# Cross attention and a feed-forward layer: the loads and conversions of the first five steps in another order, the rows of w_out written to DRAM from step 52 on, and each m made a step ahead

## The chip, the cores and the metric

The kernel runs on one core of one Trainium2 chip. The metric is the time of one execution on the device in microseconds (us), and the time of a kernel is the median of its runs. TensorE is PE in the profile, VectorE DVE, ScalarE ACT, GpSimd POOL and SyncE SP. SP computes nothing here; it issues the transfers (DMAs) one after another, so its program order is a queue.

## The reference, cut to what matters

```python
# x (8, 8, 512, 64), state (8, 8, 32, 64), w_in (512, 2048) and w_out (2048, 512)
scores = scale * np.matmul(x, state.transpose(0, 1, 3, 2))   # softmax over the 32 states
xread = np.matmul(a, state)
scores2 = scale * np.matmul(state, x.transpose(0, 1, 3, 2))  # softmax over the 512 tokens
sread = np.matmul(a2, x)
attn_out = np.concatenate([xread, sread], axis=2)            # 8 batches x 8 heads x 544 rows x 64
...
x = attn_out.transpose(0, 2, 1, 3).reshape(B * S, H * D)     # 4352 rows of 512
h = x @ w_in
g = h - np.tanh(h)
return g @ w_out
```

The weights arrive as 64-bit floats and are used as 32-bit floats.

## The kernel before, in words

**Work and chunks.** The 4352 rows are cut into nine chunks: chunks 0 to 7 are the xread rows of the eight batches, chunk 8 is all of sread. The first product is folded: instead of a·state and then w_in, the kernel makes m = state·w_in for each batch and quarter q of the 2048 hidden columns, and then h = a·m. `Chunk.hidden(f)` (L489) makes one of the 16 hidden blocks f of a chunk in a bank of `ps_h` (two banks, tiles hps), `finish` (L508) takes tanh on ACT (t) and h - tanh(h) on DVE (t or g), and `output(f)` (L526) multiplies by block f of w_out and adds up in four banks (tiles ops). Most products are made of three passes of a high and a low half (hps at L501 to L503, ops at L556 to L558); `split` (L101 to L103) makes the halves, a cast on ACT and a subtraction on DVE. Chunk 0's first blocks use plain 32-bit passes instead (hps at L499, ops at L554).

**Weights.** A block of weights is loaded raw (`Weight.load`, L111, the DMA at L121, 512 KB) and converted in four steps (`Weight.steps`, L123): a (L132, DVE), b (L133, DVE), r (L135, ACT) and p (L136, DVE, an integer addition of a and b's words and r). w00 to w03 (raw tiles w00d to w03d) are the first quarter of w_in, w10 to w33 the others, wo0 to wo15 the rows of w_out. Six raw buffers go round. `convert_win` (L617) also writes the converted quarter to the DRAM tile wf.

**m.** For batches 0 and 1 m comes from `m_first_two(q, p)` (L159): eight matmuls into a pair of banks (tiles mps, L181), then four copies on ACT (L200) into m_first (batch 0, tiles mr0) and m_second (batch 1, tiles mr1); for q of 2 and 3 batch 0's part goes to the DRAM tile md0q (L191). For batches 2 to 7 `m_units` (L208) makes it from smr and slr, two loads of state (L211, L215, split to sms and sls), with matmuls into mps (L235) and mls (L242), and writes md20 to md73 (L250, L254). `load_m` (L257) brings an m back: the DMA mr<-md (L264) into the one buffer mr, then the split to m. `Chunk.prepare(q)` calls it.

**Order.** The first part, `step(op)` (L673) over the table SEQ (L731), is laid down one engine instruction after another in the order of the table: S the scores of batch 0 (sps), c their copy, T a transpose, M a maximum, B or q the subtraction of the maximum on DVE or on POOL (L693), E exp, Z N A sum, scaling and transpose to at, a b r p the conversion steps of w00 to w03, m the products mps of a converted block, k and R the copies to mr00 and mr10 (L725, L745), h H the two halves of a hidden block of chunk 0, X its tanh and subtraction, D a matmul on a blank tile. After it comes a loop over 64 steps st (L848): chunk 0 blocks 0 to 7, chunk 1 (all 16), chunk 0 blocks 8 to 15, chunk 2, chunk 3. In each step hidden(st + 2) stands before output(st), and tables say in which step a weight is converted (CONV, WO), an m pair made (PAIRS), a row of w_out split (SPLITS) or written to the DRAM tile wod (KEEP, `keep_row`, L801, two DMAs of 256 KB a row at L805). Between the steps a scheduler orders the instructions by their dependencies, by `issue_after` (x may only stand behind y in program order) and by `high_priority`. After step 63 come two pairs of chunks (4 and 5, 6 and 7), which read w_out back from wod (L914, tiles W0m and W1m) and its mixes from wsd, and at the end chunk 8.

**Loads at the start**, in SP's order: bdr (128 KB), xT00 and xT01 (512 KB each, batch 0's x), sps (256 KB), w00d to w03d, wo0d, w10d (512 KB each).

Of the kernel before, what the change touches and what calls it, by code (L numbers as in the profile page):

```python
# [19 lines left out]
P = 128  # L20
# [17 lines left out]
def attention_ffn(ctx: ExitStack, tc: tile.TileContext, xT, xn, bd, bh, sp, sm, sl, win, wout, xout, tout, sout):  # L38
# [66 lines left out]
    class Weight:  # L105
# [33 lines left out]
        def convert(self, dst):  # L139
            for step in self.steps(dst):  # L140
                step()
# [51 lines left out]
    freed = [None]  # L193

# [61 lines left out]

    def load_m(b, q):  # L257
# [219 lines left out]
    class Chunk:  # L477
# [11 lines left out]
        def hidden(self, f):  # L489
# [7 lines left out]
            for k in range(nk):  # L497
# [133 lines left out]
    later = sorted([(s, 0, x) for s, x in zip(CONV, range(10))] + [(s, 1, x) for s, x in zip(WO, range(1, NFF))])  # L631
    loads = iter(w0[0] + wos[:1] + w0[1][:2] + [wos[x] if w else rest[x] for _, w, x in later])
# [17 lines left out]
    EARLY = int('0')  # L650
# [22 lines left out]
    def step(op):  # L673
# [18 lines left out]
        elif k in "Bq":  # L692
            o((nc.gpsimd if k == "q" else nc.vector).tensor_sub(e3(j), e3(j), ms[j].broadcast_to([P, 16, 32])))  # L693
# [7 lines left out]
        elif k in "Nw":  # L701
            o((nc.gpsimd if k == "w" else nc.vector).tensor_mul(e3(j), e3(j), zs[j].broadcast_to([P, 16, 32])))
# [3 lines left out]
        elif k in "abrp":  # L706
            if j not in csteps:
                if j % 2 == 0:
                    wb[j // 2] = pool.tile([P, 2, 512], F32, tag="wf", name=f"w00{j}", bufs=WB)
                csteps[j] = w0[0][j].steps(wb[j // 2][:, j % 2])  # L710
            x = csteps[j]["abrp".index(k)]()
            if x is not None:
                o(x)
            if k == "p":
                load(1)
                w = wb[j // 2][:, j % 2].rearrange("p (r f) -> p r f", r=4)
# [14 lines left out]
        elif k == "X":  # L731
            t = hts[j] = pool.tile([P, 512], F32, tag="t", name=f"t0_{j}", bufs=TB)
            a = nc.scalar.activation(t, hps[j], AF.Tanh)
            g = chunks[0].g[j] = pool.tile([P, 512], F32, tag="g", name=f"g0_{j}", bufs=GB)
            d = nc.vector.tensor_sub(g, hps[j], t)
            o(a)
            o(d)
            tanhs.append((a.ins, d.ins))
        elif k == "R":

            if j == 0:
                m_second[0] = second(0)
            with tc.issue_after(tanhs[RE[j]][0]):
                for c in range(2):
                    nc.scalar.copy(m_second[0][64 * c : 64 * c + 64, :, j * P : j * P + P], mps[j][64:128, c::2])  # L745

    MP = [{"a": ps_a, "o": ps_o}[x] for x in 'oaoa']
    RE = json.loads('[1, 0, 0, 1]')
    SEQ = 'S0 c0 T0 S1 D D M0 c1 q0 a0 r1 T1 D D r0 a1 E0 M1 b0 q1 E1 p0 D Z0 b1 D N0 Z1 p1 A0 N1 m0 k0 D m1 a2 k1 A1 r2 a3 h0 H0 h1 H1 b3 b2 p2 X0 X1 m2 r3 D p3 m3 k2 D k3'
# [3 lines left out]
    for j in range(4):  # L753
        step(f"R{j}")
    FILL = json.loads('[1, 0, 1, 2]')
    afters = [firstDVE[0], tanhs[0][1], tanhs[1][1]]
# [29 lines left out]
    KEEP = [32 + x for x in range(16)]  # L786
# [12 lines left out]
    wo_it = iter(range(1, NFF))  # L799
# [48 lines left out]
    for st, (i, f) in enumerate(order):  # L848
            with ExitStack() as gates:
                for x in tanhs[st - 1] if st > 6 else (first,):  # L850
                    gates.enter_context(tc.issue_after(x))
                for _ in range(CONV.count(st)):
                    convert_win(*next(convs))
                    load(1)
                for _ in range(WO.count(st)):
                    x = next(wo_it)
                    convert_wout(x, wos[x])
# [272 lines left out]
```

## Time and profile before

| what | us |
|---|---|
| median of three runs | 658.48 |
| the runs | 660.97, 658.48, 658.43 |
| the profiled execution, its own time | 658.81 |
| its span, first to last instruction | 657.0 |
| TensorE busy | 635.4 (97%) |
| DVE, ACT, POOL busy | 482.0, 384.5, 27.0 |
| mean granted TensorE clock | 0.997 of 2.4 GHz |

The span is 1.8 us shorter than the execution's own time, and that time is 0.33 us above the median. Busy time is an average over stages. A timeline row has the start, the length, the engine, the line, the operation and its tiles, and in brackets how long the engine stood idle ahead of it and who ended that.

### The profile page before, as it was taken

To read this page: it belongs to the slowest core of one execution; us is meant where nothing else is said; L and a number is where in the kernel's file an instruction comes from. 1 tells how busy PE (TensorE), PEld (TensorE's weight loads), DVE (VectorE), ACT (ScalarE), POOL (GpSimd) and SP (SyncE) were. 2 spreads that over 40 slices of the span, in tenths; PEclk is the share of its full clock that TensorE was granted. 3 is DMA by queue.
4 is the path that set the end of the run, shared out by engine and by line. 5 is a ranking of instruction groups with operands and counts; after the bars stand their busy time and mean duration, and the time that the engine had idled before them with its cause. 6 is when DMAs were issued, how large, how long until landed. Compare 5 with 4: busy or idle time off the path is not lost.

```text
span 657.0 us, 9593 instructions
## 1 busy us (share of the span) xinstructions
PE 635.4 (97%) x3450; PEld 487.0 (74%) x3450; DVE 482.0 (73%) x766; ACT 384.5 (59%) x668; POOL 27.0 (4%) x41
## 2 busy tenths in 40 slices
PE   5799899989999999999999999999999999999997
PEld 2444577767776778787878887778888888788996
DVE  5898899758547877899637777996965789754442
ACT  3775689667666566675655576445655553543532
POOL 2000000000000000000000000000000000333300
PEclk9899999999999999999999999999999999999999
DMA  8794689988879875554722446374556536899800
GB/s 310 237 384 156 212 286 361 348 290 231 276 237 286 286 223 180 210 184 155 275 103 95 161 129 223 129 217 132 151 179 187 171 121 186 293 323 355 275 7 32
DMA packets 67439, 141.21 MB, mean 215 GB/s; under 512 B 6976, under 2 KB 28736, under 8 KB 67392
## 3 DMA queue, kind: packets, MB, share of 16 engines
q1 hardware_dynamic: 64832, 132.21, 60.8%
q0 software_dynamic: 2560, 8.39, 3.6%
q8 instruction: 27, 0.44, 0.3%
q14 instruction: 20, 0.16, 0.1%
HBM read 96.01 MB, written 44.56 MB: 214 GB/s over the span
## 4 chain that ended last, share of the span: by engine, by line
PE 80%; DVE 11%; DMA 5%; issue 2%; ACT 1%; SPq 1%; ACTq 0%; DVEq 0%
PE X L965 12%; PE hps L501 8%; PE hps L502 8%; PE hps L503 8%; PE ops L556 8%; PE ops L558 8%; PE ops L557 8%; PE Y1m L965 5%; PE Y0m L965 4%; PE ops L554 3%; PE mps L235 2%; PE hps L499 2%; PE mls L242 2%; PE rps L447 1%; PE pps L426 1%
## 5 line engine op out<-in xcount | busy, mean ns | idle before, releaser
L501 PE MATMUL hps<-aT,m 128*128 128x512 f32 x240 | 95.8, 400 | 3.0 <-DVE t L521 1.7
L502 PE MATMUL hps<-aT,m 128*128 128x512 f32 x240 | 93.8, 391 | 0.0
L503 PE MATMUL hps<-aT,m 128*128 128x512 f32 x240 | 93.4, 390 | 0.0
L556 PE MATMUL ops<-wo,g 128*128 128x512 f32 x232 | 90.7, 396 | 2.1 <-ACT g L103 2.1
L557 PE MATMUL ops<-wo,g 128*128 128x512 f32 x232 | 90.2, 391 | 0.0
L521 DVE TENSOR_TENSOR t<-hps,t 128x512 f32<-128x512 f32 (+1 forms) x74 | 46.5, 628 | 46.2 <-ACT t L521 45.9
L558 PE MATMUL ops<-wo,g 128*128 128x512 f32 x232 | 78.3, 393 | 0.0
L515 ACT ACTIVATE t<-hps 128x512 f32<-128x512 f32 x64 | 38.3, 598 | 63.8 <-PE hps L503 61.5
L515 DVE TENSOR_TENSOR G<-hps,t 128x512 f32<-128x512 f32 x64 | 43.9, 687 | 38.8 <-ACT t L515 38.7
L521 ACT ACTIVATE t<-hps 128x512 f32<-128x512 f32 (+1 forms) x74 | 40.7, 553 | 45.1 <-PE hps L503 43.5
L501 PEld LDWEIGHTS hps<-aT,m 128*128 128x128 f32 x240 | 45.0, 188 | 19.1 <-DVE G L515 3.1
L103 ACT CAST g<-t 128x512 fp32r<-128x512 f32 (+1 forms) x74 | 42.2, 575 | 27.5 <-DVE t L521 27.1
L103 DVE TENSOR_TENSOR g<-t,g 128x512 fp32r<-128x512 f32 (+1 forms) x74 | 46.3, 627 | 14.6 <-ACT g L103 14.3
L556 PEld LDWEIGHTS ops<-wo,g 128*128 128x128 f32 x232 | 43.4, 188 | 15.2 <-ACT g L103 2.9
L502 PEld LDWEIGHTS hps<-aT,m 128*128 128x128 f32 x240 | 45.1, 188 | 10.6 <-issue 1.7
L503 PEld LDWEIGHTS hps<-aT,m 128*128 128x128 f32 x240 | 45.1, 188 | 9.5
L558 PEld LDWEIGHTS ops<-wo,g 128*128 128x128 f32 x232 | 43.2, 188 | 11.9 <-issue 1.2
L557 PEld LDWEIGHTS ops<-wo,g 128*128 128x128 f32 x232 | 43.6, 188 | 9.8 <-issue 0.7
L1003 POOL DMA_DIRECT2D wl<-wod x32 | 23.4, 730 | 585.1 <-DVE g1m L103 550.9
L965 PE MATMUL X<-g0m,W0m 128*128 128x512 f32 x192 | 46.9, 390 | 0.5 <-DVE g0m L103 0.5
L965 PE MATMUL X<-g1m,W1m 128*128 128x512 f32 x192 | 45.9, 390 | 0.6 <-DVE g1m L103 0.6
L103 ACT CAST g1m<-G 128x1024 fp32r<-128x1024 f32 x28 | 29.2, 1055 | 28.8 <-PE Y1m L965 12.7
(262 smaller groups left out, 1169.2 us busy)
## 6 DMA issues: line engine op xcount, KB each, us to landing
mr<-md SPq DMA_DIRECT2D x26, 512.0 KB, 4.0
xT<-in_xT SPq DMA_DIRECT2D x16, 512.0 KB, 4.7
wod<-wo SPq DMA_DIRECT2D x32, 256.0 KB, 5.1
md<-st SPq DMA_DIRECT2D x64, 128.0 KB, 3.7
xn<-in_xn SPq DMA_DIRECT2D x16, 512.0 KB, 5.0
wsd<-ws SPq DMA_DIRECT2D x16, 512.0 KB, 3.4
W0m<-wsd SPq DMA_DIRECT2D x16, 512.0 KB, 4.0
W1m<-wsd SPq DMA_DIRECT2D x16, 512.0 KB, 4.8
```

The lines of the kernel that those rows point to most:

```text
L103: return nc.scalar.copy(hi, src), (sub or nc.vector).tensor_sub(lo, src, hi)
L501: nc.tensor.matmul(ps, mhi[k][:, cols], ahi[:, k], start=(k == 0), stop=False)
L502: nc.tensor.matmul(ps, mhi[k][:, cols], alo[:, k], start=False, stop=False)
L503: made = nc.tensor.matmul(ps, mlo[k][:, cols], ahi[:, k], start=False, stop=(k == nk - 1))
L515: main(nc.scalar.activation(t, ps, AF.Tanh), nc.vector.tensor_sub(g, ps, t))
L521: tanhs.append((nc.scalar.activation(t, ps, AF.Tanh).ins, nc.vector.tensor_sub(t, ps, t).ins))
L554: return nc.tensor.matmul(o, g[:, tok], w, start=(f in self.begins), stop=stop).ins
L556: nc.tensor.matmul(o, g[:, 0, tok], w[:, 0], start=(f in self.begins), stop=False)
L557: nc.tensor.matmul(o, g[:, 0, tok], w[:, 1], start=False, stop=False)
L558: return nc.tensor.matmul(o, g[:, 1, tok], w[:, 0], start=False, stop=stop).ins
L965: made = nc.tensor.matmul(out[t], w[:, e, x, cols], y[:, e], start=first and j == 0 and e == 0 and c == 0, stop=last and j == 3 and e == 1 ...
L1003: nc.gpsimd.dma_start(wo[f][:, :, cols].bitcast(F32), wod[:, f % 2, half, f // 2])
```

## The change

Five things are changed. Loads: w00d and w01d come right behind the halves of xT0, w02d and w03d behind sps, and wo1d is among the first. SEQ: the subtraction of the maximum is on DVE (B) for both halves, wo0 and wo1 are converted inside the table (a4 to p5), tanh (X) and subtraction (x) are separate entries, and so are the copies to mr10 (R). The other conversions of the first steps are chained: each may only stand behind step b of the one before (`turn`). `m_first_two`'s matmuls stand behind the newest three-pass matmul of `hidden` (`newest`). `prepare` is called a step earlier. A row of w_out is written to wod from step 52 on, two rows a step, behind the newest load of mr (`lastmr`), where it was one row a step from step 32 on, behind the newest weight load.

```diff
         def convert(self, dst):
-            for step in self.steps(dst):
-                step()
+            return [step() for step in self.steps(dst)][1].ins
...
+                        elif newest[0] is not None:
+                            behind.enter_context(tc.issue_after(newest[0]))
                         made = nc.tensor.matmul(
                             pss[c][rows], sps[r, p - 1 + c, rows], wfs[q, k][r, c], start=True, stop=True
...
-            nc.sync.dma_start(r, mdram[b][q].rearrange("g h n f -> (h n) g f"))
+            lastmr[0] = nc.sync.dma_start(r, mdram[b][q].rearrange("g h n f -> (h n) g f")).ins
...
+                newest[0] = made.ins
...
-    CONV = [0, 0, 7, 8, 9, 10, 11, 12, 13, 14]
-    WO = [0, 1, 2, 3, 4, 5, 6, 8, 9, 10, 12, 13, 14, 15, 16]
+    CONV = [1, 1, 8, 8, 9, 10, 11, 12, 13, 14]
+    WO = [0, 2, 3, 4, 5, 6, 9, 10, 11, 12, 13, 14, 15, 16]
...
-    load(EARLY)
     nc.sync.dma_start(bdr, bd[0])
     for hf in range(2):
         nc.sync.dma_start(xrs[hf], xT[0, hf])
+        load(1)
     nc.sync.dma_start(sps, sp)
-    load(5 - EARLY)
+    load(3)
...
-        elif k in "Bq":
-            o((nc.gpsimd if k == "q" else nc.vector).tensor_sub(e3(j), e3(j), ms[j].broadcast_to([P, 16, 32])))
+        elif k == "B":
+            o(nc.vector.tensor_sub(e3(j), e3(j), ms[j].broadcast_to([P, 16, 32])))
...
-    SEQ = 'S0 c0 T0 S1 D D M0 c1 q0 a0 r1 T1 D D r0 a1 E0 M1 b0 q1 E1 p0 D Z0 b1 D N0 Z1 p1 A0 N1 m0 k0 D m1 a2 k1 A1 r2 a3 h0 H0 h1 H1 b3 b2 p2 X0 X1 m2 r3 D p3 m3 k2 D k3'
+    SEQ = 'S0 a0 c0 r0 b0 D D S1 T0 p0 M0 m0 a1 c1 B0 E0 T1 r1 b1 M1 k0 p1 D D D m1 B1 k1 r2 Z0 a2 N0 b2 D D D A0 E1 Z1 h0 p2 N1 R0 h1 A1 r4 r3 m2 R1 a3 H0 b3 k2 X0 H1 X1 p3 m3 x0 k3 R3 a4 x1 b4 R2 p4 a5 r5 b5 p5'
...
-    KEEP = [32 + x for x in range(16)]
+    KEEP = [52+x//2 for x in range(16)]
...
-            with tc.issue_after(loadlog[-1]):
+            with tc.issue_after(lastmr[0]):
                 nc.sync.dma_start(wod[:, f % 2, half, f // 2], wo[f][:, :, cols].bitcast(F32))
...
+                if st + LAG + 1 < len(order):
+                    ni, nf = order[st + LAG + 1]
+                    if nf % 4 == 0 and st > 1:
+                        chunks[ni].prepare(nf // 4)
```

DVE's program order at the start of the kernel, before (e00 and e01 are the two halves of the scores, w00d and w01d the first raw weights; POOL does the two subtractions):

```order
L688 STREAM_TRANSPOSE e00_142<-s0_140 128x512
L691 TENSOR_REDUCE m100_149<-e00_142 128x16
L132 TENSOR_SCALAR w000_153<-w00d_123 128x512
L688 STREAM_TRANSPOSE e01_158<-s0_140 128x512
L132 TENSOR_SCALAR w000_153<-w01d_125 128x512
L691 TENSOR_REDUCE m101_165<-e01_158 128x16
L133 SCALAR_TENSOR_TENSOR w000_153<-w00d_123,w000_153 128x512
L136 ISA w000_153<-w000_153,w00r_154 128x1024
```

Transpose and maximum of the first half stand ahead of the first conversion step, and no subtraction of the maximum is in the list. After the change the same place reads as follows (L697 is that subtraction):

```order
L132 TENSOR_SCALAR w000_140<-w00d_121 128x512
L133 SCALAR_TENSOR_TENSOR w000_140<-w00d_121,w000_140 128x512
L692 STREAM_TRANSPOSE e00_152<-s0_143 128x512
L136 ISA w000_140<-w000_140,w00r_141 128x1024
L695 TENSOR_REDUCE m100_158<-e00_152 128x16
L132 TENSOR_SCALAR w000_140<-w01d_124 128x512
L697 TENSOR_TENSOR e00_152<-e00_152,m100_158 128x512
L692 STREAM_TRANSPOSE e01_170<-s0_143 128x512
L133 SCALAR_TENSOR_TENSOR w000_140<-w01d_124,w000_140 128x512
L695 TENSOR_REDUCE m101_174<-e01_170 128x16
L136 ISA w000_140<-w000_140,w01r_165 128x1024
L697 TENSOR_TENSOR e01_170<-e01_170,m101_174 128x512
```

The conversion of w00 stands first, and two subtractions are new on DVE.

ACT's order around the first blocks of chunk 1, before (t1_0 is the tanh of chunk 1's block 0; mr02 and mr12 get the m pair of q = 2):

```order
L200 COPY mr02_678<-mps020_680 64x512
L200 COPY mr12_679<-mps020_680 64x512
L200 COPY mr02_678<-mps021_681 64x512
L200 COPY mr12_679<-mps021_681 64x512
L521 ACTIVATE t1_0_545<-hps1_0_538 128x512
```

The four copies stand ahead of the first tanh of chunk 1. After the change:

```order
L583 COPY ob0_21_583<-ops0_0_2_341 128x512
L525 ACTIVATE t1_0_544<-hps1_0_537 128x512
L135 ACTIVATE w22r_635<-w22d_486 128x512
L525 ACTIVATE t1_1_564<-hps1_1_557 128x512
...
L525 ACTIVATE t1_3_660<-hps1_3_653 128x512
L202 COPY mr02_669<-mps020_671 64x512
```

The four copies moved from ahead of t1_0 to behind t1_3; on TensorE the pair's eight matmuls moved from ahead of hps1_0 to behind hps1_3.

SP's order around slr and the first m that comes back from DRAM, before (md03 is written here, md02 read):

```order
L191 DMA md03_84<-mr03_887 128x2x512
L805 DMA wod_77<-wo13_927 128x2x256 x2
L215 DMA slr_1066<-in_sl 128x512
L220 DMA w101_1212<-wf0_110 128x1024
L805 DMA wod_77<-wo14_964 128x2x256 x2
...
L250 DMA md20_85<-st00_1090 32x2x512
...
L264 DMA mr02_1332<-md02_83 128x2x512
```

The load of mr02 stands behind slr, and writes of w_out (L805) between them. After the change:

```order
L222 DMA w101_1211<-wf0_110 128x1024
L192 DMA md03_84<-mr03_889 128x2x512
L268 DMA mr02_1319<-md02_83 128x2x512
L217 DMA slr_1068<-in_sl 128x512
L222 DMA w110_1358<-wf1_111 128x1024
L252 DMA md20_85<-st00_1092 32x2x512
```

No write of w_out is left here, the load of mr02 stands ahead of slr instead of behind it, and it uses the buffer that md03's write reads. The 32 writes stand in SP's order behind the loads mr31 (4 of them), mr32 (4), mr40 (12) and mr33 (12), three m of chunk 3 and the first of chunk 4.

## Rows read from the trace of the kernel before

**Rows 1.** The page, busy us of each engine over the span.

```profile
PE 635.4 (97%) x3450; PEld 487.0 (74%) x3450; DVE 482.0 (73%) x766; ACT 384.5 (59%) x668; POOL 27.0 (4%) x41
```

**Rows 2.** Three stretches: us, busy of PE, PEld, DVE, ACT, POOL, clock, DMA.

```profile
10.00:20.00 10.00, 5.70 (x31) 3.89 (x29) 9.72 (x20) 4.12 (x9) 1.43 (x1) 1.00 0.99 348
20.00:30.00 10.00, 7.94 (x29) 4.91 (x30) 8.99 (x18) 8.77 (x19) 0.00 (x0) 0.85 0.66 189
...
80.00:120.00 40.00, 40.00 (x211) 29.72 (x210) 40.00 (x69) 33.96 (x60) 0.00 (x0) 1.00 0.96 333
```

**Rows 3.** Timeline of TensorE, 0 to 60 us.

```profile
4.79 3.68 PE L680 MATMUL sps<-xT,bdr 128*64 128x512 f32 x8 [4.79 <-DMA xT<-in_xT]
...
26.15 1.26 PE L722 MATMUL mps<-w,sps 128*128 128x128 f32 x8 [2.06 <-DVE w L136]
...
28.05 3.07 PE L499 MATMUL hps<-at,mr 128*128 128x512 f32 x4
...
53.20 1.98 PE L499 MATMUL hps<-at,mr 128*128 128x512 f32 x4
```

**Rows 4.** Timeline of TensorE from 73 us on.

```profile
73.78 0.39 PE L503 MATMUL hps<-aT,m 128*128 128x512 f32 x1
...
76.30 0.50 PE L501 MATMUL hps<-aT,m 128*128 128x512 f32 x1 [1.68 <-DVE t L521]
```

**Rows 5.** Timeline of ACT from 72 us on.

```profile
72.54 2.36 ACT L200 COPY mr<-mps 64x512 f32<-64x512 f32 x4
```

**Rows 6.** Timeline of TensorE from 118 us on.

```profile
118.43 0.96 PE L235 MATMUL mps<-wst,sms 64*128 64x512 f32 x6
...
136.57 0.50 PE L556 MATMUL ops<-wo,g 128*128 128x512 f32 x1 [2.10 <-ACT g L103]
```

**Rows 7.** Timeline of ACT from 109 us on.

```profile
109.03 2.37 ACT L200 COPY mr<-mps 64x512 f32<-64x512 f32 x4
...
134.96 1.04 ACT L103 CAST m<-mr 128x1024 fp32r<-128x1024 f32 x1 [2.89 <-DMA mr<-md]
```

**Rows 8.** Timeline of SP's queue from 101 us on.

```profile
101.47 11.76 SPq L805 DMA_DIRECT2D wod<-wo  x13
...
129.68 0.43 SPq L264 DMA_DIRECT2D mr<-md  x1
```

**Rows 9.** Timeline of DVE, 9 to 26 us.

```profile
9.21 1.06 DVE L132 TENSOR_SCALAR w<-w00d 128x512 uint32<-128x512 uint32 x1 [0.36 <-DMA w00d<-in_win]
...
12.54 1.31 DVE L136 CUSTOM_DVE_ANT_0 w<-w,w00r 128x1024 uint16<-128x1024 uint16 x1
...
23.18 0.42 DVE L132 TENSOR_SCALAR w<-w11d 128x512 uint32<-128x512 uint32 x1
23.52 0.69 DVE L133 SCALAR_TENSOR_TENSOR wp<-wo0d,wp 128x512 uint32<-128x512 uint32 x1
24.12 0.69 DVE L735 TENSOR_TENSOR g<-hps,t 128x512 f32<-128x512 f32 x1
...
25.32 0.69 DVE L136 CUSTOM_DVE_ANT_0 w<-w,w03r 128x1024 uint16<-128x1024 uint16 x1
```

**Rows 10.** Timeline of POOL, 5 to 20 us.

```profile
8.94 1.05 POOL L693 TENSOR_TENSOR e<-e,m 128x512 f32<-128x512 f32 x1 [7.20 <-DVE m L691]
```

**Rows 11.** DMA issues, 100 to 131 us: KB each, us from issue to landing.

```profile
md<-mr SPq DMA_DIRECT2D x1, 512.0 KB, 4.6
...
slr<-in_sl SPq DMA_DIRECT2D x1, 256.0 KB, 4.6
```

**Rows 12.** Timeline of SP's queue, 299 to 319 us.

```profile
299.10 0.42 SPq L313 DMA_DIRECT2D bdr<-in_bh  x1
310.25 0.52 SPq L822 DMA_DIRECT2D wsd<-ws  x1
...
318.06 0.43 SPq L264 DMA_DIRECT2D mr<-md  x1
```

**Rows 13.** Timeline of ACT from 337 us on.

```profile
337.51 1.04 ACT L103 CAST m<-mr 128x1024 fp32r<-128x1024 f32 x1
```

More of the change, by code (lines that the diff above doesn't have):

```diff
@@ L290, in convert_wout @@
                 plain[f // 2] = big(f"wp{f}", [P, 2, DM], F32)
-            part.convert(plain[f // 2][:, f % 2])
-            return
+            return part.convert(plain[f // 2][:, f % 2])
         w = pool.tile([P, 512], F32, tag="c2", name=f"wor{f}", bufs=CSB)
-        part.convert(w)
+        made = part.convert(w)
         wo[f] = big(f"wo{f}", [P, 2, DM], F32R)
         split(wo[f][:, 0], wo[f][:, 1], w)
+        return made
     plain = {}
@@ L630, in attention_ffn @@
     rest = w0[1][2:] + w0[2] + w0[3]
-    later = sorted([(s, 0, x) for s, x in zip(CONV, range(10))] + [(s, 1, x) for s, x in zip(WO, range(1, NFF))])
-    loads = iter(w0[0] + wos[:1] + w0[1][:2] + [wos[x] if w else rest[x] for _, w, x in later])
+    later = sorted([(s, 0, x) for s, x in zip(CONV, range(10))] + [(s, 1, x) for s, x in zip(WO, range(2, NFF))])
+    loads = iter(w0[0] + wos[:2] + w0[1][:2] + [wos[x] if w else rest[x] for _, w, x in later])
     def load(n):
@@ L700, in step @@
             o(nc.vector.reciprocal(zs[j], zs[j]))
-        elif k in "Nw":
-            o((nc.gpsimd if k == "w" else nc.vector).tensor_mul(e3(j), e3(j), zs[j].broadcast_to([P, 16, 32])))
+        elif k == "N":
+            o(nc.vector.tensor_mul(e3(j), e3(j), zs[j].broadcast_to([P, 16, 32])))
         elif k == "A":
@@ L707, in step @@
             if j not in csteps:
[L708 to L713, printed above, removed]
+                if j > 3:
+                    if j == 4:
+                        plain[0] = big("wp0", [P, 2, DM], F32)
+                    csteps[j] = wos[j - 4].steps(plain[0][:, j - 4])
+                else:
+                    if j % 2 == 0:
+                        wb[j // 2] = pool.tile([P, 2, 512], F32, tag="wf", name=f"w00{j}", bufs=WB)
+                    csteps[j] = w0[0][j].steps(wb[j // 2][:, j % 2])
+            o(csteps[j]["abrp".index(k)]())
             if k == "p":
                 load(1)
+            if k == "p" and j < 4:
                 w = wb[j // 2][:, j % 2].rearrange("p (r f) -> p r f", r=4)
@@ L732, in step @@
             t = hts[j] = pool.tile([P, 512], F32, tag="t", name=f"t0_{j}", bufs=TB)
-            a = nc.scalar.activation(t, hps[j], AF.Tanh)
+            hts[j, 0] = nc.scalar.activation(t, hps[j], AF.Tanh)
+            o(hts[j, 0])
+        elif k == "x":
             g = chunks[0].g[j] = pool.tile([P, 512], F32, tag="g", name=f"g0_{j}", bufs=GB)
-            d = nc.vector.tensor_sub(g, hps[j], t)
-            o(a)
+            d = nc.vector.tensor_sub(g, hps[j], hts[j])
             o(d)
-            tanhs.append((a.ins, d.ins))
+            tanhs.append((hts[j, 0].ins, d.ins))
         elif k == "R":
-            if j == 0:
+            if 0 not in m_second:
                 m_second[0] = second(0)
-            with tc.issue_after(tanhs[RE[j]][0]):
-                for c in range(2):
-                    nc.scalar.copy(m_second[0][64 * c : 64 * c + 64, :, j * P : j * P + P], mps[j][64:128, c::2])
+            for c in range(2):
+                o(nc.scalar.copy(m_second[0][64 * c : 64 * c + 64, :, j * P : j * P + P], mps[j][64:128, c::2]))
     MP = [{"a": ps_a, "o": ps_o}[x] for x in 'oaoa']
-    RE = json.loads('[1, 0, 0, 1]')
-    SEQ = 'S0 c0 T0 S1 D D M0 c1 q0 a0 r1 T1 D D r0 a1 E0 M1 b0 q1 E1 p0 D Z0 b1 D N0 Z1 p1 A0 N1 m0 k0 D m1 a2 k1 A1 r2 a3 h0 H0 h1 H1 b3 b2 p2 X0 X1 m2 r3 D p3 m3 k2 D k3'
+    SEQ = 'S0 a0 c0 r0 b0 D D S1 T0 p0 M0 m0 a1 c1 B0 E0 T1 r1 b1 M1 k0 p1 D D D m1 B1 k1 r2 Z0 a2 N0 b2 D D D A0 E1 Z1 h0 p2 N1 R0 h1 A1 r4 r3 m2 R1 a3 H0 b3 k2 X0 H1 X1 p3 m3 x0 k3 R3 a4 x1 b4 R2 p4 a5 r5 b5 p5'
     for op in SEQ.split():
@@ L752, in attention_ffn @@
     chunks[0].m[0] = [m_first[0][:, k] for k in range(2)], None
[L753 to L756, printed above, removed]
     a0 = state_read(0, ss)
     late1 = late_read(1)
-    with tc.issue_after(afters[FILL[0]]):
-        convert_wout(0, wos[0])
-    load(1)
+    turn = firstDVE[0]
     for p in range(2):
-        with tc.issue_after(afters[FILL[1 + p]]):
-            convert_win(1, p)
+        with tc.issue_after(turn):
+            turn = convert_win(1, p)
         load(1)
         m_first_two(1, p)
-    first = afters[FILL[3]]
     m1 = m_units()
@@ L798, in attention_ffn @@
     pairs = iter([(1, 2), (1, 3)] + [(q, p) for q in (2, 3) for p in range(4)])
-    wo_it = iter(range(1, NFF))
+    wo_it = iter(range(2, NFF))
     def keep_row(f):
@@ L849, in attention_ffn @@
             with ExitStack() as gates:
-                for x in tanhs[st - 1] if st > 6 else (first,):
+                for x in tanhs[st - 1] if st > 6 else ():
                     gates.enter_context(tc.issue_after(x))
[L852 to L857, printed above, removed]
+                for x in [1] * CONV.count(st) + [0] * WO.count(st):
+                    with ExitStack() as order_gate:
+                        if st <= 6:
+                            order_gate.enter_context(tc.issue_after(turn))
+                        if x:
+                            made = convert_win(*next(convs))
+                        else:
+                            x = next(wo_it)
+                            made = convert_wout(x, wos[x])
+                    if st < 2:
+                        turn = made
                     load(1)
```

8 lines of the change are left out of this document (5 added, 3 removed).

## The prediction, made before the changed kernel had run

> **What bounds the kernel now.** I began with the page: TensorE is busy 635.4 of 657.0 us [rows 1], so only its 21.6 us of idle time can be won, and a wait off TensorE is worth something only if TensorE waits for it. Then the timeline of TensorE, for the places of that idle time. It waits in the first 28 us, for the first x and then for converted blocks of w_in [rows 3]; once at 76.30 for DVE's subtraction of a tanh [rows 4]; and once at 136.57 for ACT's cast of g [rows 6]. From 80 to 120 it is full, 40.00 of 40, and so is DVE [rows 2]. The table of stretches names the engine behind the first waits: DVE is busy 9.72 of the ten us from 10 to 20, TensorE 5.70 [rows 2]. The timelines of ACT, DVE and SP then say what each wait was for.
>
> **The change, part by part.** All times are on the profiled execution: span 657.0, its own time 658.81, which is 0.33 above the median.
>
> *A, the head.* Between the landing of xT00, which releases TensorE at 4.79 [rows 3], and that of w00d, which releases DVE at 9.21 [rows 9], three transfers come in: xT01 (512 KB), sps (256) and w00d (512). That is 4.4 us for 1280 KB, 1.77 for 512 KB. In the new order w00d lands at 4.8 + 1.8 = 6.6, xT01 at 8.3, w01d at 10.1. DVE can convert w00 from 6.6 on; it then does 0.34 + 3 x 0.60 for w00 and the transpose, and the maximum, and waits for w01d until 10.1. Prices on a DVE that never rests, start to start: 0.34 for L132 (23.18 to 23.52) and 0.60 for L133 and the other 128x512 forms (23.52 to 24.12) [rows 9]. From w01's first step to w03's last the new order has 23 instructions: 3 at 0.34, 16 at 0.60, 4 tiny ones on z at about 0.2 (an estimate: a third of a 0.60), 11.4 us. So w03 is done at 21.5, where its last step ended at 25.32 + 0.69 = 26.0 before [rows 9]. TensorE's products of it take 1.26 [rows 3], and the next hidden block starts at 22.9 in place of 28.05: 5.1 earlier.
>
> Here the two subtractions have come back to DVE, 2 x 0.60 = 1.2, included above. Against that stand two of DVE's rows that were long: 1.06 for an L132 which otherwise has 0.42, and 1.31 for an L136 with 0.69 [rows 9]. The first ran while POOL did its subtraction, 8.94 to 9.99 [rows 10]; I put the second down to POOL's other one. That gives back 0.64 + 0.62 = 1.3, so the move costs nothing. The Trainium skill, page "Perfetto Trace Analysis", section "Optimizing Scalar/DVE Operations", says that with DVE saturated, giving work to GpSimd may make sense, and adds that the two share a read port, so that it might not help. By the first half this part of the change would cost its 1.2; the stretched rows side with the second half.
>
> What follows on TensorE up to 53.20 holds the same products in both kernels and took 25.15 us from 28.05. In it the clock was low: 0.85 in the ten us from 20 to 30 [rows 2], 1.5 us lost, seen in 3.07 for four passes that later take 1.98 [rows 3]. At full clock it is 23.6, to 46.5. DVE is later than that: two blocks of w_out (6 x up to 0.60), the chunk's first subtractions and the start of w10 are nine instructions, 3 x 0.34 + 6 x 0.60 = 4.6, from 21.5 to 26.1; I add 1.7 for waits on ACT, busy 8.77 of ten us there [rows 2], and get 27.8. From there to the subtraction that TensorE's block at 53.20 waits for (it frees a ps_h bank) are 37 instructions: 9 at 0.34, 27 at 0.60, one of double size at 1.2, 20.5 us, to 48.3. So A = 53.2 - 48.3 = **-4.9**. Its ends: -6.7 if TensorE alone sets it (46.5), 0 if nothing of it arrives; I take -4.9, the DVE rows being the nearest. The low clock, if it comes back, is hidden in the 1.8 that TensorE waits.
>
> *B, the four copies.* At 72.54 ACT spends 2.36 on the copies of an m pair [rows 5] and starts the first tanh of chunk 1 at 74.9, though its block was done at 73.78 + 0.39 = 74.17 [rows 4]. With the pair behind block 3 the tanh goes first: **-0.75**. The pair's matmuls are paid later, no gain. Ends: 0 and -1.68, the whole wait [rows 4].
>
> From there to 118 TensorE has no gap [rows 2], so A + B arrive, if DVE, full too, is as early: its instructions are the same from there on, so it starts earlier by the same amount. With prepare a step ahead m is split earlier. I take 0 for that.
>
> *C, the wait at 136.57.* The mr02 that ACT casts at 134.96 was issued at 129.68 [rows 7, 8], on a queue where a write of a w_out row costs 11.76 / 13 = 0.90 [rows 8]. In the new order no such write is near and the load stands ahead of slr. I expect the 2.10 [rows 6] gone: **-2.1** (ends 0 and -2.1).
>
> *D, a new wait.* On SP the load of mr02 now needs md03's write to have landed, since that write reads the one mr buffer, and slr is queued behind it; ACT and DVE split slr for the first mls product. md03's copies on ACT end at 109.03 + 2.37 = 111.4 [rows 7]; 5.65 earlier by A and B, and 1.4 later because six passes of block 9 now stand ahead of the pair (6 x 0.23): 107.1. The write takes 4.6 [rows 11], so mr02 is issued at 111.7, slr at 112.2; 4.6 for slr too [rows 11] is long for a queue emptier than then, I take 4.2: 116.4, cast and split 117.1. TensorE does the mps before it at 118.43 - 5.65 = 112.8 [rows 6] and reaches mls after 0.9 and 12 passes (2.7) at 116.4. So **+0.7**; ends 0 and +5 (next part).
>
> *E, the writes of w_out.* 32 writes leave the stretch up to 131 and come behind the loads of mr31, mr32, mr40 and mr33. Between 299.52 and 310.25 SP did nothing [rows 12], which takes 11 or 12 of them. The load of mr33, issued at 318.06, is cast at 337.51 [rows 12, 13]; with the 5.3 that mr02's load took [rows 7, 8] it has 14 us to spare. Cover holds: **0**, with +3.6 as the end if the first four delay what stands behind them in full.
>
> Sum: -4.9 - 0.75 - 2.1 + 0.7 = -7.05. 658.48 - 7.05 = **651.4** on the median (span 650.0).
>
> **Rivals.**
> 1. *The subtractions cost their 1.2* because the two long rows were no work of POOL's. Against: the first lies on POOL's row. Then -5.85, 652.6. The Trainium skill's first half, above, is this case.
> 2. *SP stands at mr02 for longer, and slr with it*: md03's copies come where ACT has time, and ACT is busy 33.96 of 40 there [rows 2]. If they win nothing (111.4), slr is split at 121.4, a wait of 5.0 in place of 0.7: -2.75, 655.7. Half of it gives -4.9, 653.6, which is how I enter this case. For it: the wait at 136.57 was of this kind.
> 3. *The head gains nothing by 53*: TensorE idles more in the new head, and its granted clock, 0.85 from 20 to 30 [rows 2], stays at the low level of the two (1.2 GHz). To eat A, 4.9 and the 1.8 of cover, it would have to run at half for 13 us. Or the conversions of wo2 and wo3 come late. Then -0.75 - 2.1 + 0.7 = -2.15, 656.3, no difference.
> 4. *Slower: the writes of w_out hold up mr33.* 20 of them stand ahead of its load. They fit 10.7 us of idle queue; with 14 to spare and 7.05 won, the kernel is slower from (10.7 + 14 + 7.05) / 20 = 1.6 us a write. They took 0.90 with all else that ran then. At twice that, 1.8, it is 36 - 31.75 = +4.3: 662.8. Against: twice the price, on a queue with less in it.
> 5. *More than the sum*: A at its end of -6.7 and B at -1.68: -9.8, 648.7.
>
> **How the numbers follow.** Forecast 0.50, rival 1 0.12, rival 2 0.15, rival 3 0.14, rival 4 0.05, rival 5 0.04. A measurement of this kernel can tell about 0.5%, 3.3 us, so the limit of faster is 655.2. Forecast and rivals 1, 2 and 5 are faster: 0.81; rival 3 the same: 0.14; rival 4 slower: 0.05. The range runs from 648.7, rival 5, to 656.3, rival 3's value, so that rival 4 and half of rival 3 are left out.
>
> **What would show it.** In the new profile DVE's first L132 should start near 6.6 and w03's last step near 21; the long rows should be 0.42 and 0.69; TensorE's block that stood at 53.20 should start near 48.3, and the wait at 76.30 be about half; at 136 no wait of two us, but one of 0.7 near 116 for slr; from 140 on the same waits, 7 us earlier, with mr33's cast not moved by its load. The prediction is wrong if the wait for slr is over two us, if TensorE's clock is low beyond 30 us, if DVE's conversions of wo2 and wo3 stop TensorE before 48, or if a wait stands behind the writes of w_out past 260.

## The result, and the profile after

The changed kernel took 653.50 us (median of 6 runs, 652.55 to 654.55) where the kernel before took 660.07 on the same chip (6 runs): a ratio of 0.9892, 95% interval 0.9871 to 0.9913. Put on the 658.48 of the runs shown before, that is 651.4. Two of the kernels below also had executions of 1059 to 1624 us, which the ratios leave out. The sign, the size and the range of the forecast hold; two terms of its sum do not, the head (A) and the new wait (D), and the sections below are mostly about the first. That the forecast is met to the tenth is partly luck: the span of the profiled execution fell by 6.2 where the sum has 7.05, and a second set of runs of the same kernel, the control below, gave 0.9920, which would be 653.2.

The profiled execution took 652.6 with a span of 650.8, 6.2 less than before. Its page, to be read against [rows 1]:

```profile
PE 632.0 (97%) x3448; PEld 485.8 (75%) x3448; DVE 481.7 (74%) x768; ACT 384.8 (59%) x668; POOL 24.4 (4%) x39
```

TensorE's idle time fell from 21.6 to 18.8, its busy time by 3.4, of which the low clock from 20 to 30 before was 1.5 [rows 2]. Where its idle time lies now is told by the stretches (us, busy of PE, PEld, DVE, ACT, POOL, clock, DMA share, GB/s), against [rows 2]:

```profile
10.00:20.00 10.00, 7.45 (x39) 5.54 (x40) 9.83 (x21) 6.86 (x15) 0.00 (x0) 1.00 1.07 391
20.00:30.00 10.00, 9.99 (x31) 4.81 (x30) 8.71 (x17) 8.12 (x17) 0.00 (x0) 1.00 0.74 224
30.00:40.00 10.00, 8.17 (x38) 3.99 (x37) 9.78 (x19) 6.75 (x12) 0.00 (x0) 1.00 0.71 232
40.00:50.00 10.00, 8.49 (x52) 3.59 (x50) 8.70 (x16) 6.76 (x12) 0.00 (x0) 1.00 1.02 396
...
80.00:120.00 40.00, 40.00 (x210) 29.76 (x210) 39.90 (x68) 35.28 (x61) 0.00 (x0) 1.00 0.57 198
...
130.00:140.00 10.00, 10.00 (x46) 7.50 (x44) 4.65 (x9) 5.68 (x11) 0.00 (x0) 1.00 0.72 207
```

The stretch from 20 to 30, with 7.94 busy and a clock of 0.85 before, is full at full clock. New idle time stands from 30 to 50, 1.8 and 1.5 us. From 130 to 140 there is none left. The timeline of TensorE (start, length, line, tiles, idle ahead and its releaser) against [rows 3, 4, 6]:

```profile
23.21 3.60 PE L502 MATMUL hps<-at,mr 128*128 128x512 f32 x8
...
35.99 1.19 PE L560 MATMUL ops<-wo,g 128*128 128x512 f32 x4 [1.10 <-ACT wo L103]
37.79 0.50 PE L561 MATMUL ops<-wo,g 128*128 128x512 f32 x1 [0.61 <-DVE wo L103]
...
45.28 0.50 PE L561 MATMUL ops<-wo,g 128*128 128x512 f32 x1 [1.51 <-DVE wo L103]
...
50.43 1.98 PE L502 MATMUL hps<-at,mr 128*128 128x512 f32 x4 [0.30 <-DVE g L523]
...
71.64 0.50 PE L504 MATMUL hps<-aT,m 128*128 128x512 f32 x1 [1.02 <-DVE t L525]
...
75.61 0.50 PE L560 MATMUL ops<-wo,g 128*128 128x512 f32 x1
...
118.75 0.62 PE L244 MATMUL mls<-wst,sls 128*128 128x512 f32 x2
```

The block that stood at 28.05 starts at 23.21, that of 53.20 at 50.43; the wait of 1.68 at 76.30 is 1.02 at 71.64; the wait of 2.10 at 136.57 is gone. The waits at 35.99, 37.79 and 45.28, for the splits of w_out's rows 2 and 3 (wo, L103), are new. Behind them stands DVE:

```profile
7.23 0.43 DVE L132 TENSOR_SCALAR w<-w00d 128x512 uint32<-128x512 uint32 x1 [7.23 <-DMA w00d<-in_win]
...
21.41 0.69 DVE L136 CUSTOM_DVE_ANT_0 w<-w,w03r 128x1024 uint16<-128x1024 uint16 x1
...
28.17 0.69 DVE L525 TENSOR_TENSOR t<-hps,t 128x512 f32<-128x512 f32 x1 [0.72 <-ACT t L525]
...
43.59 0.43 DVE L132 TENSOR_SCALAR wp<-wo6d 128x512 uint32<-128x512 uint32 x1 [1.30 <-DMA wo6d<-in_wout]
...
44.54 0.69 DVE L103 TENSOR_TENSOR wo<-wor,wo 128x512 fp32r<-128x512 f32 x1
...
49.69 1.28 DVE L523 TENSOR_TENSOR g<-hps,t 128x512 f32<-128x512 f32 x2
```

The row to look at is 43.59: the first step of wo6 waits 1.30 us for its raw block, and the split of wo3 at 44.54, for which TensorE waits at 45.28, stands behind it. SP's queue says why wo6d is late, and shows the two places of the later steps:

```profile
33.12 0.90 SPq L321 DMA_DIRECT2D xT<-in_xT  x2
34.12 0.38 SPq L626 DMA_DIRECT2D wf<-w  x1
34.60 0.51 SPq L121 DMA_DIRECT2D wo6d<-in_wout  x1
...
109.51 0.37 SPq L192 DMA_DIRECT2D md<-mr  x1
112.32 0.37 SPq L268 DMA_DIRECT2D mr<-md  x1
112.78 0.42 SPq L217 DMA_DIRECT2D slr<-in_sl  x1
...
310.04 0.46 SPq L268 DMA_DIRECT2D mr<-md  x1
310.55 12.39 SPq L806 DMA_DIRECT2D wod<-wo  x12
```

wo6d is issued behind batch 1's x (xT, twice 512 KB) and a wf of 512 KB; it takes 9.0 us to land where wo5d, ahead of these, took 4.4 (last column):

```profile
wo5d<-in_wout SPq DMA_DIRECT2D x1, 512.0 KB, 4.4
wo6d<-in_wout SPq DMA_DIRECT2D x1, 512.0 KB, 9.0
```

In the kernel before, wo6d stood ahead of that x, and it landed in 5.5 us, so the change made this wait itself:

```profile
35.33 0.33 SPq L121 DMA_DIRECT2D wo6d<-in_wout  x1
...
36.18 0.90 SPq L318 DMA_DIRECT2D xT<-in_xT  x2
```

### The profile page after: what moved, and what is told of

It reads as the page before. It is cut to its first block, busy times and chain, and to the rows that moved or that the text cites. A ratio compares the mean times of both kernels' runs of the same rounds, so it can differ in the third digit from the quotient of the medians.

```text
span 650.8 us, 9590 instructions
## 1 busy us (share of the span) xinstructions
PE 632.0 (97%) x3448; PEld 485.8 (75%) x3448; DVE 481.7 (74%) x768; ACT 384.8 (59%) x668; POOL 24.4 (4%) x39
## 4 chain that ended last, share of the span: by engine, by line
PE 88%; DVE 7%; DMA 2%; issue 1%; ACT 1%; SPq 0%; ACTq 0%; DVEq 0%
PE X L975 12%; PE hps L504 9%; PE ops L560 9%; PE ops L562 9%; PE ops L561 9%; PE hps L505 9%; PE hps L506 9%; PE Y1m L975 5%; PE Y0m L975 4%; PE mps L237 2%; PE ops L558 2%; PE mls L244 2%; DMA wo6d<-in_wout 1%; PE rps L450 1%; PE pps L429 1%
## 5 line engine op out<-in xcount | busy, mean ns | idle before, releaser
L103 ACT CAST g<-t 128x512 fp32r<-128x512 f32 (+1 forms) x74 | 42.3, 575 | 27.8 <-DVE t L525 27.2
L103 DVE TENSOR_TENSOR g<-t,g 128x512 fp32r<-128x512 f32 (+1 forms) x74 | 46.2, 626 | 14.5 <-ACT g L103 14.2
L103 ACT CAST g1m<-G 128x1024 fp32r<-128x1024 f32 x28 | 29.2, 1054 | 28.9 <-PE Y1m L975 12.7
```

Source lines behind the costliest of these rows:

```text
L103: return nc.scalar.copy(hi, src), (sub or nc.vector).tensor_sub(lo, src, hi)
```

## The experiments

Each ratio is to the kernel before on the same chip, with its 95% interval.

**The control.** The changed kernel once more.

> The changed kernel itself, as the reference for the three runs beside it on the same chip. Both theories of the head expect 0.989 of the kernel before, about 653 us, and TensorE's block with the last plain tanh subtraction (50.43 in the profile of the change, 53.20 before) at 50.4.

Measured: 654.95, 0.9920 (0.9893 to 0.9947). The wait for wo6d is here too, 2.02 us, and TensorE's for the split 2.24. What is new is the clock:

```profile
45.00:50.00 5.00, 3.10 (x9) 2.20 (x10) 4.78 (x9) 3.68 (x6) 0.00 (x0) 0.84 0.96 367
50.00:55.00 5.00, 5.00 (x24) 1.71 (x23) 4.02 (x8) 2.77 (x5) 0.00 (x0) 0.82 0.92 341
```

After that wait four passes took 3.18 us where they take 1.88 in the other execution, and the block of 50.43 came at 53.35. So of the 2.9 us about 1.7 are clock (0.16 and 0.18 of five us each), 0.8 the first x, which landed at 5.58 in place of 4.79, and 0.7 the longer wait, less the 0.30 ahead of the block, which is gone here: in this execution the head won nothing up to there. In the 12 runs of the two sets the mean granted clock tells it too: the six at 1.00 took 652.55 to 653.91, the six at 0.996 or 0.997 took 653.98 to 656.29.

**Are the subtractions dear on DVE?** They go back to POOL.

```diff
-            o(nc.vector.tensor_sub(e3(j), e3(j), ms[j].broadcast_to([P, 16, 32])))
+            o(nc.gpsimd.tensor_sub(e3(j), e3(j), ms[j].broadcast_to([P, 16, 32])))
```

> Only the two subtractions of the maximum go back from DVE to POOL; nothing else moves on any engine but DVE and POOL. Forecast (the move costs nothing, since DVE's rows stretch while POOL works): the last step of w03 on DVE starts at 21.4 as in the change (within 0.4), two of DVE's rows are 0.6 longer, block at 50.4, time of the change within 0.5 us. Rival 1 (the two cost DVE their 1.2): the last step of w03 at 20.2. If in addition DVE's rows set the head to the end, the block comes at 49.2 and the time falls by 1.2; if the landing of wo6d at 43.6 sets its end, the block stays at 50.4 either way.

Measured: 653.68, 0.9917 (0.9891 to 0.9944). From w00's first step (7.55) to w03's last (21.74) it is 14.19 us, in the change 14.18. With two instructions fewer DVE is no earlier, though here 0.94 of it was a wait for ACT. The two longer rows that I expected on DVE are not there; it is POOL's second subtraction that is long, 1.43. The block came at 53.25, behind a wait of 3.04 us for the split of wo3 and with a clock of 0.79 and 0.87 from 45 to 55. So this kernel does not settle rival 1; the one with the subtractions on POOL and the x later, further down, says more.

**What the order of the loads is worth.**

```diff
         nc.sync.dma_start(xrs[hf], xT[0, hf])
-        load(1)
     nc.sync.dma_start(sps, sp)
-    load(3)
+    load(5)
```

> Only the order of the first loads is that of before (xT00, xT01, sps, w00d, w01d); the engines' orders stay. Theory (DVE starts with the landing of w00d and never catches up): DVE's first step at 9.2 in place of 7.23, the last step of w03 2.0 later at 23.4, block at 52.4, time 2 us above the change, so that 2.0 of the head's 2.8 us come from the loads. Rival (the head has slack further on, the landing of wo6d or TensorE's own work): the 2.0 is there at w03 and under 0.7 is left of it at the block.

Measured: 654.83, 0.9928 (0.9906 to 0.9950). DVE starts at 8.88, w03's last step at 23.06 (+1.65), and the block of 50.43 stands at

```profile
52.49 1.98 PE L502 MATMUL hps<-at,mr 128*128 128x512 f32 x4 [0.32 <-DVE g L523]
```

So by this pair of executions 2.06 of the head's 2.77 come from the order of the loads, 0.41 of them through a longer wait for wo6d (1.71). The other 0.71 was not taken apart: the new order in SEQ and the chained conversions had no run of their own. The medians on one chip (654.83 and the control's 654.95) do not show it: the control's runs spread over 3.3 us with their clock, and three of its six are under the lowest here, 654.55.

**Does wo6d's late landing cost the rest?** Batch 1's attention starts a step later, so that its x is loaded behind wo6d.

```diff
-        "att1": [0, 1, 2, 3, 4, 5],
+        "att1": [1, 1, 2, 3, 4, 5],
```

> Batch 1's loads (1 MB) are issued behind those of wo6d and wo7d instead of ahead of them; TensorE's and ACT's orders stay, DVE moves two rows of wo7. Theory (the head's gain was 2.1 us short of the forecast because DVE waits 1.30 us for wo6d at 43.59, which lands 9.0 us after its issue behind 1.5 MB of others): wo6d lands near 39, DVE's wait goes, TensorE's wait of 1.51 at 45.28 falls to 0.3 or less, block at 49.1, time 1.3 us below the change. Rival (wo6d is only last among several that come at about the same time, DVE's rows set the rest): under 0.4 us gained.

Measured: 652.21, 0.9886 (0.9865 to 0.9908), 2.7 below the control on the same chip. wo6d lands in 5.5 us, its step on DVE waits for nothing, and TensorE's wait for the split of wo3 is gone. The block stands at 50.07 all the same, where 49.1 was expected, since in this execution the clock fell after the waits at 36 and 38:

```profile
35.00:40.00 5.00, 3.32 (x17) 2.23 (x10) 4.80 (x9) 4.35 (x7) 0.00 (x0) 0.83 0.97 320
40.00:45.00 5.00, 5.00 (x27) 2.45 (x27) 5.00 (x11) 2.94 (x6) 0.00 (x0) 0.83 0.98 347
```

0.17 of ten us is 1.7, but not all of it would have come back: at full clock DVE's split of wo3 (43.73 here) would have stopped TensorE again. In the last kernel of this group, at full clock, the block stands 5.57 behind the start of that split (43.35, 48.92), which would put it near 49.3 here, an estimate.

**The rival: DVE's line is simply longer.** Two copies of a tile no longer needed are added to DVE behind wo0's last step; nothing reads them.

```diff
-... b4 R2 p4 a5 r5 b5 p5'
+... b4 R2 p4 V V a5 r5 b5 p5'
...
+        if k == "V":
+            o(nc.vector.tensor_copy(es[0], es[1]))
```

> The change with two more 128x512 copies on DVE ahead of the conversion of wo1 (no use is made of them): 1.2 us more for DVE's line, all else as in the change but for two half products of block 4 and 5 that TensorE does a little earlier. Theory of wo6d (from 43 us on the head is set by the landing of wo6d, not by DVE's line): the row of wo2's low half is 1.2 later (37.05 to 38.2), the row that waits for wo6d not (it waits about 1.2 less), time of the change within 0.6 us. Rival (DVE's line sets the head to its end, and the wait for wo6d only moves along with it, since its buffer is freed by DVE): everything from 27 on 1.2 later, time 1.2 above the change.

Measured: 653.23, 0.9911 (0.9890 to 0.9932), no slower. The two copies took 0.88, and the next steps are not later: DVE's waits for ACT at 26.42 and 28.17 (0.33 and 0.72 in the change) take them up. The row I had expected to move did not move, so this is no test of the line behind 28, and the unchanged time does not choose between the two theories. The late load is there again: DVE waits 2.44 for wo6d, TensorE 2.45 for the split of wo3, the clock is 0.66 from 45 to 50, and the block comes at 52.23.

Both edits together:

> The same two copies on top of batch 1's loads issued later (e8). Theory of wo6d: with that load out of the way DVE's line sets the head, so the two copies cost their 1.2 here: the subtraction of block 4's tanh starts at about 50.1 in place of 48.9, time 1.2 us above e8. Rival (TensorE's own products set the head of e8): under 0.4 us above e8.

Measured: 651.15, 0.9880 (0.9859 to 0.9901). The expected 1.2 of cost did not come: the copies again fill time in which DVE would wait for ACT at 26 to 28. The block stands at 48.98, at full clock. So in the two executions with the x later and the clock at full it comes at 48.9 to 49.0 (the next kernel is the other), and in the seven with the new first loads and wo6d behind the x it came at 50.30 to 53.35. The late load, with the clock that in some of them fell behind its wait, is what parts the two groups.

**Subtractions on POOL and batch 1's x behind wo6d.**

> Batch 1's loads later (e8) and the two subtractions of the maximum on POOL (e5). By e5, where from the second transpose to w03's last step DVE took 9.97 us instead of 10.38 with one subtraction less, each subtraction costs DVE 0.4 net: w03's last step 0.4 to 0.8 earlier than in e8, and with DVE's line setting the head the same 0.4 to 0.8 us in the time, 651.6. Rival (the forecast's: the move costs nothing, the stretched rows give it back): e8 within 0.3 us.

Measured: 651.05, 0.9868 (0.9843 to 0.9893), with runs of 650.63 to 651.35. That is the lowest median of the study. All these runs lie below the change's lowest, 652.55, but on another chip, and the intervals of the two ratios overlap. Nor does its interval part it from the kernel with the x later alone (0.9886), or from the kernel just above, which has the subtractions on DVE and two copies more and took 651.15 on the same chip. On TensorE the third new wait is 0.48, and the block stands 0.6 behind the 48.3 of the prediction:

```profile
44.11 0.50 PE L561 MATMUL ops<-wo,g 128*128 128x512 f32 x1 [0.48 <-DVE wo L103]
...
48.92 1.98 PE L502 MATMUL hps<-at,mr 128*128 128x512 f32 x4
```

w00's first step starts at 7.08 and w03's last at 21.57: 14.49 us, where it was 14.18 in the change and 14.84 with the x later, both with the subtractions on DVE. Two instructions fewer, 1.2 us, do not show. One row of DVE and one of POOL say where most of it went:

```profile
12.53 1.56 DVE L136 CUSTOM_DVE_ANT_0 w<-w,w01r 128x1024 uint16<-128x1024 uint16 x1
```

```profile
12.49 1.05 POOL L697 TENSOR_TENSOR e<-e,m 128x512 f32<-128x512 f32 x1 [1.23 <-DVE m L695]
```

DVE's addition, 0.69 elsewhere, ends 0.55 after POOL's subtraction has ended (13.54). Rival 1 falls by these rows, as far as 1.2 us go; a few tenths can hide in the spread of the three. I had expected 0.4 to 0.8 of gain against the x later alone; the 0.35 by which the stretch is shorter is within that spread.

**Do the four copies have to stand behind block 3?** The new order of the pair is taken out.

```diff
-                        elif newest[0] is not None:
+                        elif False:
                             behind.enter_context(tc.issue_after(newest[0]))
```

> The change without the rule that the matmuls of an m pair stand behind the newest three-pass matmul of hidden: the pair of q = 2 and its four copies on ACT go back ahead of chunk 1's first tanh. Forecast (part B): the first tanh of chunk 1 starts 0.75 later against its block's end, the block that stood at 71.64 at 73.4 (1.0 of it is the pair, paid there instead of later), the product that stood at 75.61 at 76.4, time 0.75 above the change. Rival (the tanh chain is not the limit there): 75.6 as in the change, and no difference.

Measured: 657.65, 0.9963 (0.9947 to 0.9979). Its profiled execution cannot be set beside the others, so the kernel ran a second time.

> The kernel of e4 again, for a profile and times that are comparable. Forecast (part B): the block that stood at 71.64 at 73.4, the product that stood at 75.61 at 76.4, and 0.75 us above the change. Rival (the free pair moves more than one tanh: the times of e4 that are near 656 to 658 are its own): a second wait of 2 us or more between 76 and 140, time 3 to 4 us above the change.

Measured: 655.92, 0.9953 (0.9936 to 0.9969). ACT does the four copies at 70.86 (2.35) and the tanh after them, and TensorE waits 2.28 where it waited 1.02, then runs at a low clock:

```profile
74.62 0.80 PE L504 MATMUL hps<-aT,m 128*128 128x512 f32 x1 [2.28 <-DVE t L525]
```

```profile
70.00:80.00 10.00, 7.72 (x39) 5.36 (x24) 6.13 (x12) 7.32 (x13) 0.00 (x0) 0.83 0.33 100
```

From the block of 50.43 (50.92 here) to the product of 75.61 (78.95 here) it takes 28.03 in place of 25.18: 2.85, of which 1.26 is the longer wait and 1.6 the clock. The part is needed. In this execution its price is nearly four times the 0.75 that I gave it, more than half of it by the clock; by the ratios it is 4.0 us against the first set of the change and 2.2 against the control, whose interval it overlaps.

**The late writes of w_out.** First the change without them: rows from step 32 on, behind the newest weight load.

```diff
-    KEEP = [52+x//2 for x in range(16)]
+    KEEP = [32 + x for x in range(16)]
...
-            with tc.issue_after(lastmr[0]):
+            with tc.issue_after(loadlog[-1]):
```

> The change with the writes of w_out where they were (one row a step from step 32 on, behind the newest weight load): only part E, and with it part C, is undone. Forecast: on SP the load of mr02 and slr stand among the writes again, ACT's cast of that m comes after a wait of about 2 us, TensorE waits about 2.1 us near 133, time 2.1 us above the change (0.992 to 0.993 of before). Rival (the earlier head, not the writes, took that wait away, since mr02's source is ready 3.6 us earlier): no wait over 0.5 us on TensorE from 80 to 140 and time as the change.

Measured: 661.36, 1.0038 (1.0024 to 1.0053): slower than the kernel before, which neither theory had. The head's gain is there up to 115 (block at 50.30, the wait of 71.64 at 71.52). Then it is lost, on TensorE:

```profile
127.67 0.73 PE L244 MATMUL mls<-wst,sls 128*128 128x512 f32 x2 [1.28 <-ACT sls L103]
...
134.30 1.65 PE L244 MATMUL mls<-wst,sls 128*128 128x512 f32 x3 [4.29 <-ACT sl L246]
```

and on SP:

```profile
106.88 10.37 SPq L806 DMA_DIRECT2D wod<-wo  x11
117.34 1.51 SPq L192 DMA_DIRECT2D md<-mr  x1
...
121.18 0.60 SPq L217 DMA_DIRECT2D slr<-in_sl  x1
...
126.99 0.38 SPq L268 DMA_DIRECT2D mr<-md  x1
```

Eleven writes stand without a pause ahead of md03's write, which goes out at 117.34 in place of 109.51, and slr and mr02 behind it 8.4 and 14.7 later than in the change. That is only 1.8, 0.7 and 2.7 us ahead of the kernel before (119.14, 121.88 and 129.68), where TensorE had won 3.56. How the 4.29 divides is not shown: ahead of the copy that ends it (ACT, sl) ACT had waited 4.16 for slr, 1.95 for DVE and 0.55 for mr02. TensorE's two waits, 5.57, are as much as C's 2.10 and the 3.56 won ahead of it together (5.66), so nothing is left of either. The clock then falls and takes 3.4 of ten us more:

```profile
130.00:140.00 10.00, 5.71 (x17) 3.68 (x16) 4.54 (x7) 6.54 (x13) 0.00 (x0) 0.66 0.89 318
```

**The late writes alone**, in the kernel before, by the same two lines the other way (and `lastmr` as in the change).

> The kernel before with one edit, the late writes of w_out behind the newest load of mr; the first 110 us of TensorE are those of before. Forecast: the wait of 2.10 us at 136.57 goes, no new one over 0.7 near 122, time 2.1 us under before, ratio 0.997. Rival (the wait moves to slr or the late writes hold up mr33): ratio 0.999 to 1.001, with a wait of about 2 us at another place.

Measured: 656.89, 0.9960 (0.9944 to 0.9976): 0.4% is 2.6 us, with C's 2.1 in the interval. The stretch of the wait is full:

```profile
130.00:140.00 10.00, 10.00 (x48) 7.24 (x47) 3.47 (x6) 6.09 (x12) 0.00 (x0) 1.00 0.70 212
```

**m a step ahead, taken out.**

```diff
-                    if nf % 4 == 0 and st > 1:
+                    if False:
```

> The change without preparing m a step ahead. In the program only 16 of the 32 writes of w_out and loads next to them change places on SP; no row of TensorE, DVE or ACT moves. Forecast: no difference, TensorE's waits those of the change to 0.2 us. Rival (the place of the writes matters): a new wait past 260.

Measured: 654.87, 0.9934 (0.9915 to 0.9952). That is not apart from the control (0.9893 to 0.9947), but just above the interval of the change's first set (up to 0.9913). All four runs had a mean clock of 0.996 or 0.997, and their 654.17 to 655.25 lie among the 653.98 to 656.29 that the change took at that clock, so no price of this part shows. On SP 16 writes of w_out change place; TensorE's waits past 60 are the change's to a quarter of a us. Ahead of that the wait for the split of wo3 is 2.42 where it was 1.51, as DVE waits longer for wo6d again (2.2).

## Why the prediction was right, and where it was not

**A, the head: -4.9 forecast, -2.8 measured** (53.20 to 50.43). Its first half held: w00d released DVE at 7.23 (forecast 6.6), w03's last step ended at 22.1 (21.5), the next hidden block stood at 23.21 (22.9), the subtraction of 28.17 at 27.8. The step that failed is "37 instructions ... 20.5 us": it took 22.26. I laid DVE's work end to end there and did not look whether what it converts had landed; in that line is wo6's first step, and its load lay behind 1.5 MB of others. 1.30 of the 1.76 too much is that wait. With the load in time the same stretch took 20.58 (28.34 to 48.92, in the kernel with the subtractions on POOL), so the prices were right and the overlap with the loads was not. With it A would have been -4.3, by the same kernel. One of my conditions for being wrong, that the conversions of wo2 and wo3 stop TensorE before 48, thus came true: it waits 1.10, 0.61 and 1.51 for their splits. In the control's execution a second came true, a low clock beyond 30 us.

**The subtractions at nothing** held. DVE's two long rows of [rows 9] are 0.43 and 0.65 in the change, and with POOL back in the work a long row is back as well. I had weighed two halves of a rule: that a saturated DVE may gain from giving work to GpSimd, and that the shared port may undo it (the Trainium skill, page "Perfetto Trace Analysis", section "Optimizing Scalar/DVE Operations"). Here the second holds: 14.49 against 14.18 and 14.84.

**B, the copies: -0.75 forecast, -0.8 measured.** The product that stood at 79.17 before is at 75.61, 3.56 earlier, of which 2.77 is the head's.

**C: -2.1 forecast, -2.1 measured** in the trace, and 2.6 in the times where the late writes stand alone.

**D, the new wait for slr: +0.7 forecast, 0 measured.** mr02 went out at 112.32 (111.7) and slr at 112.78 (112.2), near the forecast by luck: md03's write was issued at 109.51, 2.4 later than I had worked out, and landed in 2.8 us, not in 4.6. The step that failed is that 4.6: I took it from the queue of before, full of writes [rows 11], and made the allowance for an emptier queue for slr alone (4.2; it took 3.7):

```profile
md<-mr SPq DMA_DIRECT2D x1, 512.0 KB, 2.8
```

```profile
116.55 0.62 ACT L103 CAST sls<-slr 128x512 fp32r<-128x512 f32 x1
```

The cast ends at 117.17, and TensorE came to the first mls at 118.75, 1.6 us to the good: The 1.8 that the write won and the 0.5 that slr won turn the forecast wait of 0.7 into that room. It is not because the head had won 2.1 less than forecast. In the kernel with the subtractions on POOL the head won 1.5 more, and md03's write (108.00), slr (111.28) and the cast came earlier by as much; mls again stands 1.6 behind the end of the cast, without a wait:

```profile
115.01 0.62 ACT L103 CAST sls<-slr 128x512 fp32r<-128x512 f32 x1
...
117.26 0.62 PE L244 MATMUL mls<-wst,sls 128*128 128x512 f32 x2
```

Rival 2 falls with it: SP stood 2.8 us at mr02, not longer than forecast.

**E, the late writes: 0 forecast, 0 measured.** mr33 is issued at 310.04, ahead of 12 of the writes, and cast at

```profile
331.28 1.04 ACT L103 CAST m<-mr 128x1024 fp32r<-128x1024 f32 x1
```

21 us later; so rival 4 was far off. Where the writes stand without a pause one took 1.03 us (12.39 for 12), not the 1.6 that this rival needed. A late wait on TensorE that stands past 400 is 6.25 earlier than before, unchanged in length.

Sum: -2.8 - 0.8 - 2.1 = -5.7 against -6.2 in the span. The 0.5 that is left lies between 118 (3.44 earlier than before, then 2.10) and 186 (6.02 earlier); it stands in no row of idle time, and I leave it open. Rival 3, that the head gains nothing, was right in part by its second form, the late conversions; in the control's execution, with the clock low as in its first form, the block stood at 53.35.

**The parts are not a sum.** I priced the late writes at C's 2.1 and called the rest of them free. Without them the span is 8.7 longer than the change's: 5.57 in two waits, and 3.4 of clock. They were what let the head's gain arrive. The sum has no term for this, and it came out near the measurement because the change has both parts, and because A's shortfall of 2.1 was made up in part by D's 0.7, which did not come, and by the 0.5 left open.

## What to carry to other kernels

When an engine's work is laid end to end to place what follows, look up for every raw block in that line when its load lands, behind what it was issued, and not only how long the instructions take. A queue with one order for all transfers holds later stages back when it is full: behind eleven writes in a row the loads came 0.7 to 2.7 us earlier where TensorE had won 3.56, and without the writes they moved with it. A gain ahead of such a queue arrives only if what those stages load is issued earlier as well, so price such parts together. Try the cheapest repair in the order of the loads: moving batch 1's x behind wo6d took the wait out and gave 652.21, and 651.05 and 651.15 in the two kernels built on it.

## What the runs showed of the hardware

Some of DVE's instructions wait out one of POOL's, and others do not. Before, L132 ended at 10.27 and L136 at 13.85, 0.28 and 0.54 after POOL's subtractions had ended (9.99 in [rows 10], and 13.31); with the subtractions on POOL, L136 ended 0.55 after (14.09 to 13.54). A transpose of DVE that ran in that kernel's first subtraction (10.11 to 11.27) took 0.71 at 10.50, as elsewhere. Where DVE had begun first, POOL's row is the longer one, 1.43 in place of 1.05: in the first try with POOL L136 began at 13.57 and the subtraction at 13.73, and before the second subtraction began behind an L133 of 11.72:

```profile
11.88 1.43 POOL L693 TENSOR_TENSOR e<-e,m 128x512 f32<-128x512 f32 x1 [1.89 <-DVE m L691]
```

The Trainium skill, page "SBUF — State Buffer", section "SBUF: two separate sides", says that the port pair the two engines share is an exclusive lock for the whole instruction, taken by whichever starts first, by DVE in a two-port mode or, against a GpSimd instruction that reads SBUF, with two inputs in SBUF. The rows agree: L136 has two inputs, the transpose one. L132 has one input, and 0.42 where the other forms of its size have 0.69, which would go with such a mode; no run shows the mode itself.

The granted clock fell towards the lower of its two levels (1.2 GHz) after short waits of TensorE, in some executions of a program and not in others. After 1.10 and 0.61 us of waits near 36 it was 1.00 in the change and 0.83 over the next ten us with batch 1's x later, where the waits were 1.10 and 0.59. After 2.24 (the control) and 2.28 (the copies) it was 0.82 to 0.84, after 1.28 and 4.29 it was 0.66; after 1.91 (the old order of the loads) it stayed 1.00. Each fall cost 1.6 to 3.4 us, 0.6 to 1.0 of the waits ahead of it, so that a wait taken away can pay nearly twice, and executions of one kernel differ by two us.
